# Four unit-matrix products into an unread bank behind each step of the last three half chunks

## The chip, the cores and the metric

The kernel runs on one core of a Trainium2 chip, whose five engines work side by side: TensorE (PE in the profile, with its weight loads as PEld), VectorE (DVE), ScalarE (ACT), GpSimd (POOL) and SyncE (SP), which only issues DMAs here. Each engine takes its instructions strictly in the order in which they are written, and starts one when the semaphores that it waits for have come. TensorE writes its results into eight banks of PSUM memory, from which VectorE and ScalarE read them.

The metric is the device time of one execution in microseconds. The profile also gives, for each stretch of time, the clock that TensorE was granted, as a share of its full speed; that share is called the clock here.

## The reference

A recurrence over 768 time steps for 4 x 8 heads of dimension 40, and behind it a gated MLP on its output:

```python
for t in range(S):
    y[:, :, t] = np.einsum('bhd,bhde->bhe', rt, state)
    Sa = np.einsum('bhde,bhe->bhd', state, at)
    state_decay = state * wt[:, :, None, :] - np.einsum('bhd,bhe->bhde', Sa, bt)
    state = state_decay + np.einsum('bhd,bhe->bhde', vt, kt)
...
h = x @ w_in
h = 0.5 * h * (1.0 + np.tanh(c * (h + 0.044715 * h ** 3)))
u, v = (h[..., :d_ff // 2], h[..., d_ff // 2:])
v_n = (v - mu) / np.sqrt(var + 1e-06) * g_ln
v_s = np.einsum('ts,bsd->btd', w_sg, v_n) + b_sg[None, :, None]
return (x + (u * v_s) @ w_out).astype(np.float32)
```

`x` is the recurrence's output, 4 x 768 x 320; `w_in` is 320 x 1024, `w_sg` 768 x 768, `w_out` 512 x 320.

## The kernel before

**Chunks.** The recurrence is worked in 12 chunks of 64 time steps (`NCH`, `C`). Within a chunk it becomes products of small matrices for each of the 4 batches, with a triangular inverse ahead of them. The state that goes from chunk to chunk lies in `sc`.

**Half chunks.** The function `half(c, hf, side)` writes one half of a chunk: two batches' steps of chunk `c`, and the output steps of two batches whose state steps came half a chunk earlier. Half number 2c + hf counts them; 22 and 23 are the halves of the last chunk (c = 11), and 24 holds only the last two batches' output steps. The steps are:

- `chain1`: TensorE makes `ru` from `at` and `vs`; ScalarE copies it to `rhsb`.
- `chain_t`: TensorE transposes the state into `tp`; ScalarE copies it to `s2`.
- `chain2`: TensorE multiplies `xt`, the inverse, by `rhsb` into the second part of the same `ru`; ScalarE writes the negative to `vu`.
- `chain3`: the new state (`sp`, left out in the last chunk), and `vu` transposed into `ut`; ScalarE copies it to `vut`.
- `chain4`: TensorE makes `pq` from `vut` and `rt`; VectorE masks it into `pqs`.
- `chain5`: TensorE makes `yp` from `pqs`, `kbt`, `s2` and `rt`; VectorE scales it into `yt`, and SyncE stores it.

Each step has a place, a number in `CH`; the steps and the list `side` are sorted by place and written in that order, and this is the order in which every engine works. `side` brings what lies between: the inverse (`gp`, `xp`, `xt`), the decoding of the MLP's weights from 64-bit floats into two 32-bit parts (`stg`, `sc`, `lt`, `wih`, `wil`, `woh`, `wol`: loads on SyncE, then ScalarE, five VectorE steps each, GpSimd), and in half 24 the first three products of the MLP (`hv`). In half 24 the steps on `w_out` fill VectorE's queue.

**Behind the halves** comes the MLP: `hv` and `hu` (the two sides of `h`), then `sg` (the product with `w_sg`), then `op` (the product with `w_out`), in an order given by `SEQ`.

**Banks.** `ps(name)` gives the next PSUM tile. From the second half of chunk 9 on all eight banks are in use (six in one pool, two in another). A step that takes a bank waits until the bank's last reader is done.

**Precision.** The recurrence's products are 32-bit floats; the profile shows two rows for each such product, and the built order one.

Of the kernel before, what the change touches and what calls it, by code (L numbers as in the profile page):

```python
# [69 lines left out]
REST = 8  # L70
SGS = (5, 3, 5, 6, 7, 8, 8, 11, 10, 11, 12, 11)
PO = 313.2
DECO = (332.0, 334.0, 336.0, 338.5, 340.5, 342.5, 344.5, 347.0)
DSTEPO = (-4.0, -1.0, 0.0, 0.7, 1.4, 2.4)
SGE = "GVGVGVGVVVGG"
# [44 lines left out]
def engines(tc):  # L120
    nc = tc.nc
    return tuple(InOrder(tc, e) for e in (nc.vector, nc.scalar, nc.gpsimd, nc.tensor, nc.sync))
# [6 lines left out]
def attention(tc, a, xd, flag, keep, ps, mlp=None):  # L129
# [3 lines left out]
    V, A, G, T, Q = engines(tc)  # L133
    with ExitStack() as ctx:

        def pool(nm, side):

            c = ctx.enter_context(ExitStack())
            return c.enter_context(tc.tile_pool(name=nm, bufs=1, side=side)), c.close

        st, _ = pool("at_static", "left")
        ring_b, _ = pool("at_ring_b", "left")
# [19 lines left out]
        ident = st.tile([128, 128], F32, name="ident")  # L162
        mask = st.tile([128, C], F32, name="mask")
        n = NP * (C + 1)
# [72 lines left out]
        def ent(c, b):  # L237
            return (4 * c + b) % RING
# [154 lines left out]
        def load_vb(c, f):  # L393
            if c < NCH:
                Q.dma_start(out=vss[f][0:64], in_=a["vb"][c, f])

        def load_vu(c, f):
            if c < NCH:
                Q.dma_start(out=vus[f][0:64], in_=a["vs"][c, f])

        def load_rv(c, f):
            if c < NCH:
                for h in range(2):
                    r = slice(D * h, D * h + D)
                    Q.dma_start(out=rts[f][r, :, h], in_=a["rt"][c, f, r])
                Q.dma_start(out=vuts[f][0:2 * D, :, :, 0], in_=a["vt"][c, f])

        def chain1(c, b):
            at, vs, rb = ats[ent(c, b)], vss[b // 2][:, b % 2], rhsb[b]
            ru = rus[b] = ps("ru")  # L410
            k = 128 if c else 64
            for p in range(NP):
                for h in range(2):
                    T.matmul(ru[64 * h:64 * h + 64, D * p:D * p + D], lhsT=at[0:k, p, h],
                             rhs=vs[0:k, p, h], start=True, stop=True, skip_group_check=True)
            A.copy(out=rb, in_=ru[:, 0:NP * D].rearrange("p (q x) -> p q x", x=D))

        def chain_t(c, b):
            if c:
                tp = ps("tp")  # L420
                for g in range(2):
                    T.transpose(out=tp[0:80, 128 * g:128 * g + 128], in_=scs[b][:, 2 * g:2 * g + 2], identity=ident)
                st2[b] = st.tile([128, 4, D], F32, name="s2", bufs=4)
                A.copy(out=st2[b][0:80], in_=tp[0:80, 0:256].rearrange("p (g x) -> p g x", x=C)[:, :, 0:D])

        def chain2(c, b):
            xt, ru, rb, vu = xts[c % 2], rus[b], rhsb[b], vus[b // 2][:, b % 2]
            for p in range(NP):
                for h in range(2):
                    r = slice(64 * h, 64 * h + 64)  # L430
                    T.matmul(ru[r, 160 + D * p:160 + D * p + D], lhsT=xt[r, 4 * b + p], rhs=rb[r, p],
                             start=True, stop=True, tile_position=(64 * h, 64 * h), skip_group_check=True)
            uv = ru[:, 160:320].rearrange("p (i g x) -> p i g x", i=2, g=2)
            for h in range(2):
                A.mul(out=vu[64:128, :, h], in_=uv[64 * h:64 * h + 64], mul=-1.0)

        def chain3(c, b):
            kbt, vu, vs, sc = kbts[ent(c, b)], vus[b // 2][:, b % 2], vss[b // 2][:, b % 2], scs[b]
            if c < NCH - 1:
                sp = ps("sp")  # L440
                for p in range(NP):
                    for h in range(2):
                        l0 = 2 * D * p + D * h
                        T.matmul(sp[64 * h:64 * h + 64, D * p:D * p + D], lhsT=kbt[:, l0:l0 + 64],
                                 rhs=vu[:, p // 2, h, p % 2], start=True, stop=True)
                cn = exs[ent(c, b)][:, :, C:C + 1]
                e = 64 + D
                ts = sp[0:e, 0:NP * D].rearrange("p (q x) -> p q x", x=D)
                V.tensor_tensor(out=ts, in0=ts, in1=sc[0:e], op=ALU.add)
                V.tensor_tensor(out=sc[0:e], in0=ts, in1=bc(cn[0:e], [e, NP, D]), op=ALU.mult)  # L450
                for h in range(2):
                    r = slice(64 * h, 64 * h + 64)
                    A.copy(out=vs[64:128, :, h], in_=sc[r])
            ut = ps("ut")
            for g in range(4):
                T.transpose(out=ut[0:80, C * g:C * g + C], in_=vu[64:128, g // 2, g % 2], identity=ident[64:128, 64:128])
            A.copy(out=vuts[b // 2][0:80, b % 2, :, 1], in_=ut[0:80, 0:256].rearrange("p (q t) -> p q t", q=4))

        def chain4(c, b):
            rt, vut = rts[b // 2][:, b % 2], vuts[b // 2][:, b % 2]  # L460
            pq = ps("pq")
            for g in range(4):
                T.matmul(pq[:, 128 * g:128 * g + 128], lhsT=vut[:, g], rhs=rt[:, :, g], start=True, stop=True)
            pqs = pqt[b] = st.tile([128, 2 * NP, C], F32, name="pqs", bufs=2)
            V.tensor_tensor(out=pqs, in0=pq.rearrange("p (q t) -> p q t", t=C),
                            in1=mask.unsqueeze(1).broadcast_to([128, 2 * NP, C]), op=ALU.mult)

        def chain5(c, b):
            kbt, rt, pqs = kbts[ent(c, b)], rts[b // 2][:, b % 2], pqt[b]
            yp = ps("yp")  # L470
            for p in range(NP):
                o = slice(C * p, C * p + C)
                for h in range(2):
                    l0 = 2 * D * p + D * h
                    T.matmul(yp[64 * h:64 * h + 64, o], lhsT=kbt[:, l0:l0 + 64], rhs=pqs[:, 4 * (p // 2) + 2 * h + p % 2],
                             start=True, stop=True, skip_group_check=True)
                for h in range(2 if c else 0):
                    T.matmul(yp[64 * h:64 * h + D, o], lhsT=st2[b][0:80, 2 * (p // 2) + h],
                             rhs=rt[0:80, p % 2, 2 * (p // 2) + h],
                             start=False, stop=True, skip_group_check=True)  # L480
            yt = st.tile([128, NP, C], F32, name="yt", bufs=2)
            V.tensor_tensor(out=yt, in0=yp[:, 0:256].rearrange("p (q t) -> p q t", t=C),
                            in1=exs[ent(c, b)][:, :, 0:C], op=ALU.mult)
            xv = xd[b, :, C * c:C * (c + 1)].rearrange("(q h e) t -> h e q t", h=2, e=D)
            for h in range(2):
                Q.dma_start(out=xv[h], in_=yt[64 * h:64 * h + D])

        def half(c, hf, side):

            p, q = 2 * hf, 2 * hf + 1  # L490
            o, r = 2 - 2 * hf, 3 - 2 * hf
            oc = c - 1 if hf == 0 else c
            st = []
            z = CH[hf]
            if c < NCH:
                if (c, hf) != (0, 0):
                    st += [(z[0], lambda: chain1(c, p)), (z[1], lambda: chain1(c, q))]
                st += [(2, lambda: load_vb(c + 1, hf)),
                       (z[2], lambda: chain_t(c, p)), (z[3], lambda: chain2(c, p)), (z[4], lambda: chain_t(c, q)),
                       (z[5], lambda: chain2(c, q)), (z[6], lambda: chain3(c, p)),  # L500
                       (z[7], lambda: (chain3(c, q), load_vu(c + 1, hf)))]
            if oc >= 0:
                st += [(z[8], lambda: chain4(oc, o)), (z[9], lambda: chain4(oc, r)),
                       (z[10], lambda: chain5(oc, o)), (z[11], lambda: (chain5(oc, r), load_rv(oc + 1, 1 - hf)))]
            for _, f in sorted(st + side, key=lambda x: x[0]):
                f()

# [104 lines left out]
class Mlp:  # L612
# [273 lines left out]
    def side(self, c, hf):  # L886

        def at(p, f):
            plan.append((p, f))

        plan = []
        if self.plan is None:
# [9 lines left out]
            for k in range(12):  # L902
                for i, d in enumerate(DSTEP[DEC[k][1]]):
                    at(max(PIN + 0.1, DEC[k][0] + d), lambda k=k, i=i: step(k, i))
            at(PO, self.open_out)
            outs = {}
# [5 lines left out]

            for k, p in enumerate(DECO):
                for i, d in enumerate(DSTEPO):
# [171 lines left out]
```

## Time and profile before

| what | value |
| --- | --- |
| time, median of 3 runs | 664.4 us (663.64 to 666.62) |
| the profiled execution's own time | 665.51 us |
| its span, first to last instruction | 663.8 us |
| instructions | 22411 |
| TensorE busy | 580.4 us, 87% |
| VectorE busy | 510.4 us, 77% |
| ScalarE busy | 391.8 us, 59% |
| GpSimd busy | 385.9 us, 58% |
| mean clock over the span | 0.900 |

The span is split into 40 slices of 16.6 us on the page, and the clock of each is given as one digit, in tenths. A row of a timeline has the start, the length, the engine, the line, the operation, what is written and read, the shapes, the number of instructions merged into it, and in brackets the engine's idle time before and who ended it. All engine calls go through one helper, so all rows have its line, and the names tell them apart.

### The profile page before, as it was taken

Reading aid. Unit: us, or ns where it says so; the run is one execution under the profiler, and the core shown is the slowest. Engines: PE = TensorE matmul, PEld = TensorE weight load, DVE = VectorE, ACT = ScalarE, POOL = GpSimd, SP = SyncE. Lnnn points to the kernel's source line nnn. Section 1 sums busy time; section 2 is a strip of 40 time slices with the busy share of each in tenths; the row PEclk is TensorE's granted clock in tenths of the full one; section 3 lists DMA queues with packets and bytes.
Section 4 is the critical chain, followed back from the end, with each engine's and each line's share of the span. In section 5 each row is a group of like instructions: output and inputs, shape, how many; then the busy total and the mean of one; then the engine's idle time right before and its main releaser. Section 6 shows DMA issues by size and latency. Waiting matters only on the chain.

```text
span 663.8 us, 22411 instructions
## 1 busy us (share of the span) xinstructions
PE 580.4 (87%) x8950; PEld 525.7 (79%) x8950; DVE 510.4 (77%) x1097; ACT 391.8 (59%) x1106; POOL 385.9 (58%) x869
## 2 busy tenths in 40 slices
PE   6547998989999899998978692969999999999996
PEld 5436787878888778887967682859999999999995
DVE  7875778989889898898777569788679668667732
ACT  5555687978878788797763744654245335424410
POOL 6588886787877878778782455464332433333321
PEclk8555599999999999999978676789999999999999
DMA  6722233443443433433344332331002002100001
GB/s 223 235 78 78 81 95 104 114 118 102 115 109 107 121 106 108 108 93 101 81 113 119 90 88 73 93 110 47 31 13 91 12 19 68 35 31 1 31 24 41
DMA packets 57617, 56.54 MB, mean 85 GB/s; under 512 B 35936, under 2 KB 47456, under 8 KB 57504
## 3 DMA queue, kind: packets, MB, share of 16 engines
q1 hardware_dynamic: 57504, 55.02, 28.9%
q8 instruction: 72, 1.18, 0.7%
q14 instruction: 41, 0.34, 0.2%
HBM read 47.14 MB, written 7.86 MB: 83 GB/s over the span
## 4 chain that ended last, share of the span: by engine, by line
PE 50%; DVE 24%; ACT 14%; issue 7%; DMA 3%; POOL 1%; SPq 1%; DVEq 0%; POOLq 0%; ACTq 0%
PE sg L115 14%; PE op L115 7%; PE hu L115 5%; PE hv L115 5%; PE ab L115 4%; DVE at L115 3%; PE pq L115 3%; DVE fixed L115 3%; PE sp L115 2%; PE ru L115 2%; ACT nts L115 2%; DVE ex L115 2%; ACT xt L115 2%; PE yp L115 2%; DVE kb L115 2%
## 5 line engine op out<-in xcount | busy, mean ns | idle before, releaser
L115 POOL TENSOR_TENSOR tg<-x,n 128x126 f32<-128x126 f32 (+21 forms) x348 | 127.9, 368 | 45.6 <-DVE n L115 7.2
L115 POOL TENSOR_TENSOR x<-x,tg 128x126 f32<-128x126 f32 (+21 forms) x348 | 133.4, 383 | 27.3
L115 POOL TENSOR_TENSOR gx<-g,gy 128x384 fp32r<-128x384 f32 x32 | 33.4, 1046 | 84.6 <-ACT gy L115 83.5
L115 PE MATMUL ab<-at,kb 64*64 64x64 f32 x1536 | 44.5, 248 | 30.6 <-DVE kb L115 17.2
L115 PE MATMUL sg<-wsh,vh 128*128 128x384 f32 x192 | 65.4, 340 | 4.3 <-ACT vh L115 4.3
L115 ACT ACTIVATE nts<-ab 32x256 f32<-32x256 f32 x192 | 62.0, 323 | 10.4 <-DVE at L115 8.0
L115 PEld LDWEIGHTS ab<-at,kb 64*64 64x64 f32 x1536 | 35.9, 155 | 40.4 <-ACT junk L115 14.0
L115 PE MATMUL sg<-wsh,vl 128*128 128x384 f32 x192 | 65.5, 341 | 1.9 <-POOL vl L115 1.9
L115 PE MATMUL sg<-wsl,vh 128*128 128x384 f32 x192 | 65.1, 339 | 0.0
L115 PE MATMUL pq<-rt,vut 128*128 128x128 f32 x384 | 60.5, 306 | 3.8 <-ACT vut L115 3.0
L115 PE MATMUL yp<-pqs,kbt 128*64 128x64 f32 x768 | 50.2, 236 | 14.6 <-DVE pqs L115 13.1
L115 ACT CAST gy<-g 128x384 fp32r<-128x384 f32 x32 | 16.4, 514 | 74.5 <-DVE g L115 74.5
L115 PEld LDWEIGHTS pq<-rt,vut 128*128 128x128 f32 x384 | 52.3, 211 | 7.0 <-ACT vut L115 3.1
L115 PEld LDWEIGHTS yp<-pqs,kbt 128*64 128x64 f32 x768 | 40.7, 147 | 18.0 <-DVE pqs L115 13.7
L115 ACT COPY vs<-sc 64x160 f32<-64x160 f32 x88 | 28.3, 321 | 38.6 <-DVE sc L115 37.7
L115 ACT CAST vh<-v 128x512 fp32r<-128x512 f32 x24 | 14.9, 621 | 55.2 <-DVE v L115 55.2
L115 PE MATMUL yp<-rt,s 80*40 80x64 f32 x704 | 46.4, 232 | 0.0
L115 DVE SCALAR_TENSOR_TENSOR g<-sg,gl,bt 128x384 f32<-128x384 f32 x32 | 19.7, 616 | 32.2 <-PE sg L115 28.4
L115 POOL TENSOR_TENSOR vl<-v,vh 128x512 fp32r<-128x512 f32 x24 | 31.3, 1305 | 22.7 <-ACT vh L115 22.7
L115 DVE TENSOR_TENSOR at<-ab,mask 64x256 f32<-64x256 f32 x96 | 35.9, 409 | 7.6 <-PE ab L115 7.3
L115 PE MATMUL ru<-rhsb,xt 64*64 64x40 f32 x768 | 32.3, 242 | 9.9 <-ACT xt L115 9.9
L115 POOL TENSOR_TENSOR rs<-rs,mhalf 128x1 f32<-128x1 f32 x24 | 13.4, 560 | 46.8 <-DVE rs L115 41.8
(135 smaller groups left out, 1658.9 us busy)
## 6 DMA issues: line engine op xcount, KB each, us to landing
main<-main SPq DMA_DIRECT2D x88, 160.8 KB
vu<-vs SPq DMA_DIRECT2D x24, 160.0 KB
vs<-vb SPq DMA_DIRECT2D x24, 160.0 KB
rt<-rt SPq DMA_DIRECT2D x48, 80.0 KB
vut<-vt SPq DMA_DIRECT2D x24, 160.0 KB
xd<-yt SPq DMA_DIRECT2D x96, 40.0 KB
xt<-xd SPq DMA_DIRECT2D x16, 192.0 KB
out<-y SPq DMA_DIRECT2D x16, 192.0 KB
```

What stands on the lines that cost most here:

```text
L115: return self.tc.keep_in_program_order(f(*a, **k))
```

## The change

A new function takes a bank and multiplies the unit matrix by itself into it, `n` times. In the halves 22, 23 and 24 it is put behind every step of the half's own list, at the step's place plus 0.001; the list `side` stays without it. That list also holds the place of a load (`load_vb`), which in half 22 and 23 gets its fill as well: 13, 13 and 4 fills of four products. Nothing reads the banks that they write.

```diff
+FILLED = (22, 23, 24)
+FILL = 4
...
+        def fill(n):
+
+            wp = ps("wp")
+            for _ in range(n):
+                T.matmul(wp[:, 0:128], lhsT=ident, rhs=ident, start=True, stop=True, skip_group_check=True)
+
...
                        (z[10], lambda: chain5(oc, o)), (z[11], lambda: (chain5(oc, r), load_rv(oc + 1, 1 - hf)))]
+            if 2 * c + hf in FILLED:
+                st += [(x + 0.001, lambda: fill(FILL)) for x, _ in st]
             for _, f in sorted(st + side, key=lambda x: x[0]):
                 f()
```

Only TensorE's order changes; the other engines' instructions are the same in the same order. Three places are shown. In these rows a number behind a name tells tiles of one name apart, and a bracket names the semaphores (`Activation` is ScalarE's, `PE` TensorE's own, `DMAHW` a DMA queue's).

TensorE in half 22, from the first `pq` to `chain2` of the first batch. Before:

```order
L115 MATMUL pq_7528<-rt1_125,vut1_130 128x128 [waits DMAHW0_49,DMAHW6_49,DVE_49,DMAHW7_49,PE_49,Activation_49]
L115 MATMUL pq_7528<-rt1_125,vut1_130 128x128 x3
L115 MATMUL tp_7537<-ident_92,sc0_120 80x128 x2
L115 MATMUL xp_7542<-xt1_90,gs0_119 32x32 [waits Activation_49]
L115 MATMUL xp_7542<-xt1_90,gs0_119 32x32 x31
L115 MATMUL tp_7577<-ident_92,sc1_121 80x128 [waits DVE_49]
L115 MATMUL tp_7577<-ident_92,sc1_121 80x128
```

Now:

```order
L117 MATMUL pq_7543<-rt1_125,vut1_130 128x128 [waits DMAHW6_49,DMAHW0_49,DMAHW7_49,DVE_49,Activation_49]
L117 MATMUL pq_7543<-rt1_125,vut1_130 128x128 x3
L117 MATMUL wp_7550<-ident_92 128x128 [waits Activation_49]
L117 MATMUL wp_7550<-ident_92 128x128 x3
L117 MATMUL tp_7557<-ident_92,sc0_120 80x128 [waits PE_49]
L117 MATMUL tp_7557<-ident_92,sc0_120 80x128
L117 MATMUL wp_7562<-ident_92 128x128 x4
L117 MATMUL xp_7567<-xt1_90,gs0_119 32x32 x32
L117 MATMUL tp_7602<-ident_92,sc1_121 80x128 [waits DVE_49]
L117 MATMUL tp_7602<-ident_92,sc1_121 80x128
```

`wp_7550` takes the bank that the last `ut` of the half before held; what it waits for on ScalarE is the copy of that `ut` into `vut`. `tp` and `xp` stand behind it.

TensorE in half 23, from `chain4` of one batch to `chain4` of the other. Before:

```order
L115 MATMUL pq_7736<-rt0_124,vut0_129 128x128 x4
L115 MATMUL ru_7711<-rhsb2_117,xt1_90 64x40 x8
L115 MATMUL ru_7724<-rhsb3_118,xt1_90 64x40 x8
L115 MATMUL tp_7778<-ident_92,sc2_122 80x128 x2
L115 MATMUL pq_7783<-rt0_124,vut0_129 128x128 x4
```

Now:

```order
L117 MATMUL pq_7816<-rt0_124,vut0_129 128x128 x4
L117 MATMUL wp_7823<-ident_92 128x128 x4
L117 MATMUL ru_7776<-rhsb2_117,xt1_90 64x40 x8
L117 MATMUL wp_7846<-ident_92 128x128 x4
L117 MATMUL ru_7794<-rhsb3_118,xt1_90 64x40 x8
L117 MATMUL wp_7866<-ident_92 128x128 x4
L117 MATMUL tp_7873<-ident_92,sc2_122 80x128 x2
L117 MATMUL wp_7878<-ident_92 128x128 x4
L117 MATMUL pq_7883<-rt0_124,vut0_129 128x128 x4
```

Four fills now stand between the two `pq`, and four more between the second `pq` and the first `yp`.

TensorE at the end of half 24, where the last `yp` is followed by the MLP's first `hu`. Before:

```order
L115 MATMUL yp_8085<-pqs_8048,kbt15_112 64x64 x2
L115 MATMUL yp_8085<-rt1_125,s2_7797 40x64 x2
L115 MATMUL hu_8133<-xh_7267,wih_6815 128x384 x3
L115 MATMUL hu_8133<-xh_7267,wil_6816 128x384 x3
L115 MATMUL hu_8133<-xl_7268,wih_6815 128x384 x2
```

Now:

```order
L117 MATMUL yp_8230<-pqs_8183,kbt15_112 64x64 x2
L117 MATMUL yp_8230<-rt1_125,s2_7902 40x64 x2
L117 MATMUL wp_8251<-ident_92 128x128 x4
L117 MATMUL hu_8283<-xh_7267,wih_6815 128x384 x3
L117 MATMUL hu_8283<-xh_7267,wil_6816 128x384 x3
L117 MATMUL hu_8283<-xl_7268,wih_6815 128x384 x2
```

One fill stands between the two.

## The prediction, before the run

> **What bounds the kernel now.** I read the page's head and slices first, then the stretches of the last half chunks, then TensorE's timeline in them, and last what ScalarE (ACT) and VectorE (DVE) do there.
>
> ```profile
> span 663.8 us, 22411 instructions
> PEclk8555599999999999999978676789999999999999
> ```
>
> The clock row is what matters: from slice 24 on the granted clock sags, and stays low for six slices of 16.6 us. The halves that the change fills lie there. By the names in the timeline they run from 361.38 (first `ru` of chunk 11) to 381.95, to 393.31, and to 417.59 (the first `hu`); the next two rows are the gated MLP.
>
> ```profile
> 361.38:381.95 20.57, 12.85 (x227) 11.48 (x224) 10.48 (x29) 13.18 (x36) 6.68 (x9) 0.73 0.35 99
> 381.95:393.31 11.36, 11.36 (x161) 10.34 (x157) 6.17 (x19) 5.99 (x19) 5.39 (x8) 0.59 0.35 95
> 393.31:417.59 24.28, 11.43 (x108) 9.87 (x105) 22.45 (x53) 9.36 (x27) 15.48 (x26) 0.74 0.23 65
> 417.59:447.07 29.48, 23.35 (x108) 20.78 (x106) 23.48 (x50) 17.30 (x39) 15.03 (x18) 0.85 0.36 106
> 447.07:663.80 216.73, 210.28 (x1153) 201.89 (x1153) 145.43 (x283) 78.56 (x159) 68.86 (x70) 0.99 0.11 35
> ```
>
> The columns are length, then busy time of PE, its weight loads, DVE, ACT, POOL, then clock. Three limits follow each other: in half 22 PE has 7.7 us of pauses, in half 23 it has none (at 0.59), in half 24 DVE is busy 22.45 of 24.28 us and PE less than half. Behind 447 PE is busy to the end, so what is late there ends late.
>
> ```profile
> 362.40:365.40 3.00, 0.06 (x3) 0.00 (x0) 1.03 (x4) 1.44 (x4) 0.00 (x0) 1.00 0.23 74
> 369.50:370.50 1.00, 0.00 (x0) 0.00 (x0) 0.39 (x2) 0.72 (x4) 0.92 (x3) 1.00 0.53 119
> 370.50:371.50 1.00, 0.00 (x0) 0.00 (x0) 1.00 (x3) 0.10 (x1) 0.51 (x1) 0.63 0.34 97
> 373.47:389.98 16.51, 16.51 (x193) 15.45 (x194) 8.24 (x22) 8.90 (x27) 7.20 (x11) 0.50 0.28 80
> 415.68:421.00 5.32, 5.32 (x43) 5.16 (x44) 4.27 (x10) 2.19 (x8) 3.68 (x8) 0.50 0.17 37
> 421.00:423.00 2.00, 2.00 (x11) 2.00 (x10) 1.76 (x3) 0.63 (x2) 0.00 (x0) 0.76 0.70 210
> ```
>
> A 3.00 us pause left the clock at 1.00; the next one began at 368.29 and the clock fell in it at about 370.8. Then PE ran 16.51 us without a pause at 0.50. That is the cold stretch that the fills could remove.
>
> **The change, part by part.**
>
> *Price of a fill.* Thirty fills of four 128x128 products are added (13, 13 and 4). The same shape in this kernel is `pq`, four products, eight rows:
>
> ```profile
> 361.38 1.08 PE L115 MATMUL ru<-vs,at 128*64 128x40 f32 x32
> 365.43 1.16 PE L115 MATMUL pq<-rt,vut 128*128 128x128 f32 x8 [2.97 <-ACT vut L115]
> 366.42 0.38 PE L115 MATMUL tp<-ident,sc 128*80 128x128 f32 x2
> 366.74 1.20 PE L115 MATMUL xp<-xt,gs 64*32 64x32 f32 x64
> 367.87 0.42 PE L115 MATMUL tp<-ident,sc 128*80 128x128 f32 x2
> 372.87 0.43 PE L115 MATMUL ru<-rhsb,xt 64*64 64x40 f32 x2 [4.58 <-ACT xt L115]
> 373.47 1.93 PE L115 MATMUL ru<-rhsb,xt 64*64 64x40 f32 x30 [0.17 <-ACT xt L115]
> ```
>
> From start to next start (365.43 to 366.42) a group costs 0.99 us at full clock. At half clock:
>
> ```profile
> 375.90 2.07 PE L115 MATMUL pq<-rt,vut 128*128 128x128 f32 x8
> 377.90 0.65 PE L115 MATMUL ut<-ident,vu 64*80 64x64 f32 x4
> ```
>
> 2.00 us. I take 0.99 and 2.00. Bounds: from below the streaming alone, by the nearest row that is wide,
>
> ```profile
> 398.66 0.84 PE L115 MATMUL hv<-wil,xh 128*128 128x512 f32 x3
> 399.34 0.62 PE L115 MATMUL hv<-wih,xl 128*128 128x512 f32 x2
> ```
>
> where three rows of 512 columns take 0.68 us, so 128 columns 0.057 and eight rows 0.45 us; from above 1.16 us, `pq`'s whole row, if each fill drained before the next instruction. `pq` is the nearest by far: same shape, type and count.
>
> The Trainium skill ("TensorE: Matmul & The Clock Gate", section "Back-to-back issue gap") gives about 81 ns for each 128-column matmul in a stream of weight loads and matmuls; eight would be 0.65 us, an estimate from that page, against the 0.99 us that this trace shows. It is one of the rivals, below.
>
> *Up to 373.47: the fills hide, nearly.* Half 22 opens with two `ru` and three fills: 361.38 + 2 x 0.5 + 3 x 0.99 = 365.35, and `pq` could not start before 365.43 anyway. Its new bank also waits for the first of the two DVE steps on `yp`, and the fill behind it takes the bank that the last `ut` held and waits for ACT's copy out of it, the third of these rows:
>
> ```profile
> 365.01 0.37 ACT L115 COPY vut<-ut 80x256 f32<-80x256 f32 x1
> 365.74 0.75 DVE L115 TENSOR_TENSOR yt<-yp,ex 128x256 f32<-128x256 f32 x2
> 367.89 0.37 ACT L115 COPY vut<-ut 80x256 f32<-80x256 f32 x1
> ...
> 372.25 1.17 ACT L115 COPY xt<-xp 32x512 f32<-32x512 f32 x2
> ```
>
> So `pq` starts at about 366.1 (365.74 and half of 0.75) and is through at 367.1, and PE stands until 368.26, with two `tp`, `xp` and two more fills queued behind that one: 368.26 + 3 x 0.99 + 1.13 (`xp`) + 2 x 0.32 (`tp`) = 373.0. `xp` itself ends at about 371.6, before ACT comes to copy it (372.25, held by a decode step of DVE), so `ru` still starts on ACT's time. **Nothing gained, nothing lost**, but the pauses are now 0.7 and 1.2 us, and by the rows above the clock should not fall.
>
> *From 373.47 on PE is the limit, and pays.* Until the second `pq` of half 23 ends there were 16.51 us at 0.50: 8.26 at full clock, a gain of 8.25. In the same stretch the order puts 14 fills: 14 x 0.99 = 13.86. The end moves from 389.98 to 373.47 + 8.26 + 13.86 = 395.59, **5.6 us late**. DVE stood waiting for just that:
>
> ```profile
> 390.02 0.69 DVE L115 TENSOR_TENSOR pqs<-pq,mask 128x512 f32<-128x512 f32 x1 [2.06 <-PE pq L115]
> ...
> 394.89 0.41 DVE L115 TENSOR_TENSOR yt<-yp,ex 128x256 f32<-128x256 f32 x1
> ...
> 414.95 0.68 DVE L115 TENSOR_TENSOR pqs<-pq,mask 128x512 f32<-128x512 f32 x1
> ```
>
> From there DVE needs 4.87 us to `yt`, so it comes to it at 400.5. `yp` is behind four more fills: before, PE took 2.33 us from 389.98 to the first `yp`'s end (about 392.3, half of the two that fill the time to 393.31); at the clock of 0.81 it had there, that is 1.9. 395.59 + 4 x 0.99 + 1.9 = 401.45. So `yt` moves from 394.89 to 401.5: **6.6 us**. DVE works in order, and every later decode step and MLP step stands behind it.
>
> *Half 24 carries it.* PE enters it at 401.45 + 2 x 0.99 + 0.93 = 404.4, 11.1 late, but there DVE is the limit and PE has slack: the first `hv` ends at 406.3, ACT reads it at 401.33 + 6.6 = 407.9; the others have more. So the delay stays at 6.6, not 11.1, and the last `pqs`, at 414.95 before, starts at 421.5. The fills there cost nothing, except the last:
>
> ```profile
> 415.68 1.98 PE yp L115 x32
> 417.66 2.87 PE hu L115 x8
> ...
> 420.62 0.50 ACT p L115
> ...
> 421.21 0.55 DVE q L115
> ```
>
> This is the chain. PE still pauses some 6 us before the last `yp`, so it is cold again, and a fill now stands between `yp` and `hu`: 2.00 us. By the row of 421.00 to 423.00 (0.76) the clock rose at about 421.96, 6.28 us after PE restarted; if it does so again, `yp` 1.98, fill 2.00, then 2.3 us of `hu` cold and the other 0.57 at double speed: `hu` ends 6.6 us after the restart in place of 4.9: **1.6 us**.
>
> **Sum:** 0 + 6.6 + 0 + 1.6 = 8.2 us. The profiled execution took 665.51 us (span 663.8), so 673.7. It lies 1.1 over the median of 664.4; I put the forecast against the median: **672.6 us**.
>
> Other parts: the bank numbers shift by 30 allocations; PE's new waits for its own earlier fills were over long before, but for one fill directly behind another in the same bank, in front of a pause. ACT, DVE, POOL and SP keep their order. The three loads and stores that half chunks issue stay where they are.
>
> **Rivals.**
>
> *Fills are cheap, no change.* The point is where 373.47 + 8.26 + 14f = 389.98, f = 0.59 us. With 0.65 us: 390.83 at `pqs`, 0.85 late, `yp` in time; the cold fill 1.3. Together 2.15 us: 666.6. Against it stands the 0.99 row; for it, that the four fills share one matrix, which no group in the trace does.
>
> *Faster.* At f = 0.45 the cold stretch's gain wins: `pqs` ends PE's work at 388.03, 1.95 us early, DVE follows. If the fills also held the clock over half 24, `yp` and `hu` would take half of 4.85, less a fill of 0.45: another 1.95 early. 664.4 - 3.9 = 660.5. It needs the lower bound and a clock held through the 6 us pause; the trace lost it in pauses of 4.6.
>
> *The clock falls all the same.* If bank waits add pauses, fills run at 2.00 us: three of them ahead of `ru` make it 4 us late, then 16.51 + 14 x 2.00 up to `pqs`, 32 us late, near 700 with the rest. The Trainium skill speaks for it (same page, "A second HAM failure mode: psum-queue depth-cycling"): cycling through banks lets the PE idle briefly, so that the clock oscillates. Here the pauses before 373 are shorter than the 3.00 us that kept it.
>
> *Half 24 follows PE, not DVE.* Then 11.1 + 1.6: 677.1; with f = 1.16, 14.5 + 1.9: 680.8.
>
> *It does nothing.* Were the unread products not issued, 664.4; the built order shows all 30 groups.
>
> **How the numbers follow.** Forecast with its own bounds, half 24 following PE among them (668 to 681): 0.77. Cheap fills 0.11, nothing issued 0.01, faster 0.06, cold fills 0.05. 0.5% (3.3 us) is about what a measurement of this kernel can tell from no change. Slower 0.82, same 0.12, faster 0.06. The range runs from the cheap fills to most of the PE-bound half: 666.0 to 679.5.
>
> **What would show it.** `wp<-ident` rows with some 0.99 us a group at full clock; a clock of 1.00 through half 22 and 23; half 23 longer than 11.36 us though warm; `pqs` waiting for PE near 395.6; half 24 still with DVE over 90% busy and shorter PE pauses; a cold fill before `hu`. It is wrong if a group costs under 0.6 us, if the clock still falls near 371, or if the MLP's start moves by much other than 8 us.

## The result and the profile after

| | before | changed |
| --- | --- | --- |
| time, median of 4 runs each on the same chip | 664.14 us (663.64 to 666.62) | 675.71 us (673.18 to 676.99) |
| the profiled execution's own time | 665.51 us | 676.76 us |
| mean clock over the span | 0.900 | 0.92 |

The changed kernel is slower: ratio 1.0146, with a 95% interval of 1.0106 to 1.0186, which is 7 to 12 us. A second measurement on another chip ("changed again", below) gave 1.0162 (1.0137 to 1.0187). Forecast were 672.6 us and a range of 666.0 to 679.5.

The page of the changed kernel, in the same rows as before, and with its chain of work:

```profile
span 675.0 us, 22891 instructions
PEclk9555599999999999999959999788999999999999
PE 60%; DVE 16%; ACT 15%; issue 6%; DMA 2%; POOL 1%; DVEq 0%; SPq 0%; POOLq 0%; ACTq 0%
PE sg L117 14%; PE hu L117 7%; PE op L117 6%; PE hv L117 6%; PE ab L117 6%; PE wp L117 4%; PE sp L117 4%; ACT nts L117 3%; PE ru L117 3%; PE pq L117 3%; DVE at L117 2%; ACT xt L117 2%; PE yp L117 2%; PE gp L117 2%; DVE fixed L117 2%
```

The clock row has lost most of its sag: slices 20 to 28, 978676789 before, now read 959999788. The fall in slice 21 (337 to 354 us) lies ahead of the first fill; then comes full clock, and the 788 is the end of half 24 and the start of the MLP. And yet the span is 11.2 us longer. The last row says why: `wp`, the product that nobody reads, stands on the chain that ended last with 4% of the span. An instruction without a reader is on that chain only because TensorE does its queue in order and was the bound.

The five stretches, cut nearly as before: first `ru` of chunk 11, last `yp` of half 22 done, first `hv`, first `hu`, and the gated MLP. Two cuts lie a little beside the earlier ones: the last fill of half 22 (1.09 us from 385.30) is counted with half 23, and the event that was at 447.07 is at 457.40 here, 0.6 us ahead of the last cut.

```profile
362.21:385.30 23.09, 21.79 (x322) 19.60 (x318) 10.19 (x28) 13.81 (x37) 7.79 (x11) 1.00 0.32 89
385.30:406.80 21.50, 21.50 (x272) 20.01 (x269) 10.07 (x26) 7.60 (x23) 7.91 (x12) 1.00 0.26 67
406.80:427.94 21.14, 15.13 (x140) 13.59 (x138) 18.97 (x47) 8.87 (x27) 12.94 (x25) 0.82 0.20 56
427.94:458.00 30.06, 23.62 (x109) 20.87 (x109) 22.39 (x46) 16.26 (x36) 13.58 (x14) 0.84 0.37 106
458.00:675.00 217.00, 210.56 (x1153) 202.17 (x1151) 144.15 (x281) 78.05 (x157) 68.85 (x70) 0.99 0.11 34
```

Halves 22 and 23 have a clock of 1.00 (0.73 and 0.59 before), as the change is built to give. Half 23 is nevertheless 21.50 us long in place of 11.36 (20.4 without that fill), and PE is busy for all of it: at 1.00 in place of 0.59 it has much more to do. Half 24 is still DVE's: 18.97 of 21.14 us, 90%.

TensorE's timeline of the changed kernel, at two places (start, length, then the row):

```profile
372.47 1.06 PE L117 MATMUL wp<-ident 128*128 128x128 f32 x8
373.46 0.30 PE L117 MATMUL ru<-rhsb,xt 64*64 64x40 f32 x2
374.06 0.66 PE L117 MATMUL ru<-rhsb,xt 64*64 64x40 f32 x14 [0.30 <-ACT xt L117]
374.65 1.16 PE L117 MATMUL wp<-ident 128*128 128x128 f32 x8
375.74 0.66 PE L117 MATMUL ru<-rhsb,xt 64*64 64x40 f32 x16
376.33 1.16 PE L117 MATMUL wp<-ident 128*128 128x128 f32 x8
...
424.30 0.48 PE L117 MATMUL yp<-pqs,kbt 128*64 128x64 f32 x4 [6.01 <-DVE pqs L117]
426.21 2.08 PE L117 MATMUL wp<-ident 128*128 128x128 f32 x8
...
430.64 0.73 PE L117 MATMUL hu<-xh,wih 128*128 128x384 f32 x3
```

From start to next start a fill takes 1.09 us with small products on both sides (374.65 to 375.74) and 0.99 us with one on one side only (372.47 to 373.46); the last, cold one is shown with 2.08 us. PE's pauses in the first group are gone, but for 0.30 us. VectorE's timeline of the changed kernel gives the milestones to compare:

```profile
366.32 0.75 DVE L117 TENSOR_TENSOR yt<-yp,ex 128x256 f32<-128x256 f32 x2
391.65 0.69 DVE L117 TENSOR_TENSOR pqs<-pq,mask 128x512 f32<-128x512 f32 x1 [5.81 <-PE pq L117]
397.91 0.69 DVE L117 TENSOR_TENSOR pqs<-pq,mask 128x512 f32<-128x512 f32 x1 [4.17 <-PE pq L117]
403.87 0.43 DVE L117 TENSOR_TENSOR yt<-yp,ex 128x256 f32<-128x256 f32 x1 [1.03 <-PE yp L117]
423.57 0.68 DVE L117 TENSOR_TENSOR pqs<-pq,mask 128x512 f32<-128x512 f32 x1
```

DVE waits for `pq` 5.81 and 4.17 us here, where it waited 2.92 and 2.06 us before (at 385.87 and 390.02). One more row of the kernel before is needed as the partner of the last TensorE row above, the second group of `hu`:

```profile
420.32 1.16 PE L115 MATMUL hu<-xh,wih 128*128 128x384 f32 x3
```

### The profile page after: what moved, and what is told of

It reads as the page before. It is cut to its first block, busy times and chain, and to the rows that moved or that the text cites. A ratio compares the mean times of both kernels' runs of the same rounds, so it can differ in the third digit from the quotient of the medians.

```text
span 675.0 us, 22891 instructions
## 1 busy us (share of the span) xinstructions
PE 603.4 (89%) x9190; PEld 547.1 (81%) x9190; DVE 509.2 (75%) x1097; ACT 392.0 (58%) x1106; POOL 385.5 (57%) x869
## 4 chain that ended last, share of the span: by engine, by line
PE 60%; DVE 16%; ACT 15%; issue 6%; DMA 2%; POOL 1%; DVEq 0%; SPq 0%; POOLq 0%; ACTq 0%
PE sg L117 14%; PE hu L117 7%; PE op L117 6%; PE hv L117 6%; PE ab L117 6%; PE wp L117 4%; PE sp L117 4%; ACT nts L117 3%; PE ru L117 3%; PE pq L117 3%; DVE at L117 2%; ACT xt L117 2%; PE yp L117 2%; PE gp L117 2%; DVE fixed L117 2%
## 5 line engine op out<-in xcount | busy, mean ns | idle before, releaser
L117 PE MATMUL ab<-at,kb 64*64 64x64 f32 x1536 | 43.8, 245 | 31.7 <-DVE kb L117 17.8
L117 ACT ACTIVATE nts<-ab 32x256 f32<-32x256 f32 x192 | 62.0, 323 | 10.3 <-DVE at L117 7.8
L117 PE MATMUL pq<-rt,vut 128*128 128x128 f32 x384 | 57.8, 297 | 1.0 <-DVE yt L117 0.9
L117 PE MATMUL yp<-pqs,kbt 128*64 128x64 f32 x768 | 48.2, 230 | 7.5 <-DVE pqs L117 6.0
L117 PEld LDWEIGHTS pq<-rt,vut 128*128 128x128 f32 x384 | 49.9, 202 | 4.0 <-DVE yt L117 1.4
L117 PE MATMUL yp<-rt,s 80*40 80x64 f32 x704 | 44.4, 226 | 0.0
L117 DVE TENSOR_TENSOR pqs<-pq,mask 128x512 f32<-128x512 f32 x48 | 32.7, 681 | 15.0 <-PE pq L117 15.0
L117 PEld LDWEIGHTS sg<-wsh,vh 128*128 128x128 f32 x192 | 36.9, 192 | 5.8 <-ACT vh L117 5.7
```

The source lines that it names most:

```text
L117: return self.tc.keep_in_program_order(f(*a, **k))
```

## The experiments

The theory: fills cost TensorE their full time on the stretch where it is the bound, and that is more than the held clock gives back. Rivals: the price is in waits for banks or in issuing, not in the products; the held clock alone would pay; the cold fill ahead of `hu` is the main loss. All kernels are variants of the changed one, and each is timed beside the kernel before, on the same chip. Since the executions of one program differ in when the clock rises, the traces are compared by VectorE's milestones, in microseconds behind the first `yt` of half 22 (start to start): the second `pqs` of half 23, the `yt` behind it, and the last `pqs`.

| run | time, median | ratio to before (95%) | second `pqs` | `yt` | last `pqs` |
| --- | --- | --- | --- | --- | --- |
| before | 664.14 | | 24.28 | 29.15 | 49.21 |
| before again | 666.41 (one) | | 20.56 | 27.39 | 48.10 |
| changed | 675.71 | 1.0146 (1.0106 to 1.0186) | 31.59 | 37.55 | 57.25 |
| changed again | 676.94 | 1.0162 (1.0137 to 1.0187) | 31.59 | 37.54 | 57.60 |
| six fills, pauses of half 22 | 666.11 | 1.0002 (0.9976 to 1.0029) | 21.26 | 29.72 | 49.85 |
| half 24 only | 666.69 | 0.9999 (0.9973 to 1.0026) | 24.28 | 29.17 | 50.06 |
| two products a fill | 670.28 | 1.0063 (1.0040 to 1.0086) | 27.05 | 31.91 | 52.96 |
| one thin product a fill | 670.02 | 1.0069 (1.0046 to 1.0091) | 27.28 | 32.14 | 52.71 |
| two fills in half 22 | 664.57 | 0.9978 (0.9959 to 0.9996) | 20.30 | 26.97 | 47.76 |
| 9 and 24 products in half 24 | 665.58 | 0.9992 (0.9973 to 1.0012) | 20.59 | 27.39 | 48.21 |
| 16 and 28 products in half 24 | 665.10 | 0.9980 (0.9954 to 1.0007) | 24.28 | 29.17 | 50.05 |
| eight products a fill | 698.18 (one) | | 49.55 | 59.08 | 79.67 |

In the three kernels whose fills lie in half 24 alone, the first two milestones are reached without any fill, so these executions stand beside "before" and "before again" as three more of the same program up to there. Of the five, three have the second `pqs` at 24.28 and two at 20.56 and 20.59: by this much one program's executions differ, and the comparisons below with "before" are with one of the first kind.

### Only the fills in the pauses of half 22

```diff
-FILLED = (22, 23, 24)
+FILLED = (22,)
...
-                st += [(x + 0.001, lambda: fill(FILL)) for x, _ in st]
+                st += [(x + 0.001, lambda: fill(FILL)) for x, _ in st if x < 5.2]
```

> Only the first six fills of half 22 stay, those that are written ahead of the 372.87 step; the other 24 are left out. Theory A (a fill costs PE about 1.0 us, and what the fills bring is a clock that does not fall at 371): the six hide in the pauses as they do in the changed kernel, the stretch of 16.5 us at half clock takes about 8.3, and VectorE, which has 8.2 us of work there, follows by 5 to 8 us: 656.5 to 659.5 us. Rival B (the small products of the recurrence cannot hold the clock, only fills among them do): the clock falls again inside half 22 or 23, 661 to 665 us. Rival C (the loss is in the new waits for banks in half 22, not in the products): slower than before, 667 us or more.

No change was measured: 666.11 against 666.26 us. The gain that the theory expected isn't there, though the clock did what it was to do, without any fill behind 375.3. The windows of this kernel's trace:

```profile
375.00:385.00 10.00, 8.58 (x188) 7.71 (x186) 7.56 (x18) 6.63 (x20) 3.97 (x5) 1.00 0.19 58
385.00:398.00 13.00, 11.40 (x120) 9.26 (x117) 9.71 (x21) 5.56 (x17) 7.80 (x11) 1.00 0.39 104
```

So the kernel's own products, most of them small, held the clock here once it was up. Where the gain went shows in the milestones: the second `pqs` is 3.0 us earlier than before, the `yt` behind it 0.6 us later. TensorE's and then VectorE's timeline of this kernel:

```profile
365.48 0.61 PE L117 MATMUL ru<-vs,at 128*64 128x40 f32 x16
...
375.28 1.28 PE L117 MATMUL ru<-rhsb,xt 64*64 64x40 f32 x32
```

```profile
365.64 0.75 DVE L117 TENSOR_TENSOR yt<-yp,ex 128x256 f32<-128x256 f32 x2
...
386.90 0.68 DVE L117 TENSOR_TENSOR pqs<-pq,mask 128x512 f32<-128x512 f32 x1
388.89 0.95 DVE L117 TENSOR_SCALAR sc<-sc 128x256 f32<-128x256 f32 x2 [1.31 <-ACT sc L117]
392.44 0.62 DVE L117 TENSOR_SCALAR sc<-sc 128x256 f32<-128x256 f32 x2 [1.74 <-ACT sc L117]
395.36 0.41 DVE L117 TENSOR_TENSOR yt<-yp,ex 128x256 f32<-128x256 f32 x1
```

Two things ate it. PE came into half 22 at 365.48 here (at 361.38 in the trace of before), so six fills no longer fitted ahead of `chain2`, which starts 9.64 us behind the first `yt` (375.28 - 365.64) in place of 7.13. And DVE, having its `pqs`, stands 1.31 and 1.74 us for a decode step of ACT. This kernel's chain of work says for what the second of these steps waits (start, length, piece):

```profile
387.13 0.72 POOL lt L117
...
388.93 2.97 DMA stg<-w_out
391.98 0.44 ACT sc L117
```

GpSimd frees a staging buffer, SyncE's load into it takes 2.97 us, and only then do ACT and DVE go on. TensorE has no part in these pieces.

### Only the fills of half 24

```diff
-FILLED = (22, 23, 24)
+FILLED = (24,)
```

> Only the four fills of half 24 stay. Theory A: three of them hide in PE's pauses there, the last one stands between the last yp and the first hu at half clock and costs 1.5 to 2 us: 665.5 to 666.2 us, and the first hu group ends 6.5 us after the last yp begins (4.9 before). Rival (this fill warms the clock early enough to pay for itself): within 0.5 us of before, hu ends under 5.5 us after yp begins.

The time can't tell 1.5 us from nothing here; the trace can. TensorE's rows of this kernel at the end of half 24:

```profile
416.22 0.48 PE L117 MATMUL yp<-pqs,kbt 128*64 128x64 f32 x4 [7.03 <-DVE pqs L117]
418.13 2.08 PE L117 MATMUL wp<-ident 128*128 128x128 f32 x8
...
422.12 0.70 PE L117 MATMUL hu<-xh,wih 128*128 128x384 f32 x3
```

From the last `yp` to the second group of `hu` it is 422.12 - 416.22 = 5.90 us, against 420.32 - 415.68 = 4.64 before and 430.64 - 424.30 = 6.34 in the changed kernel. In the second execution of the changed kernel ("changed again") it is 431.50 - 426.07 = 5.43. The cold fill thus costs 0.8 to 1.7 us, by when the clock rises. It is a loss, but the small one.

### Two products a fill, and eight

```diff
-FILL = 4
+FILL = 2
```

> All 30 fills, but two products each in place of four, so about 0.52 us each at full clock; same banks, same waits. Theory A: at 0.59 us a fill the gain of the clock and the products' price cancel at the second mask of half 23, so this one is about 1 us early there, and about 0.8 us late by the cold fill before hu: 662.5 to 665.5 us. Rival C (the waits for banks are what costs): as slow as the changed kernel, 672 to 677 us. Rival D (the clock brings nothing on the path, the products cost half): 668 to 671 us.

It was slower by 4 us, where the time of before or a little less was expected: half the products don't turn the loss into a gain. The time lies in the range of the rival by which the clock brings nothing on the path (668 to 671), but the trace speaks against that rival. Of the 2.8 us by which the second `pqs` is later, 1.7 are there when `chain2` starts (374.59, 8.85 us behind the first `yt`), and only 1.1 come between, where 14 fills of 0.45 us for the products alone (below) would have added 6.3 had the clock brought nothing. TensorE's first fill inside `chain2`, and VectorE's second `pqs`, of this kernel:

```profile
375.78 0.71 PE L117 MATMUL wp<-ident 128*128 128x128 f32 x4
392.79 0.69 DVE L117 TENSOR_TENSOR pqs<-pq,mask 128x512 f32<-128x512 f32 x1 [2.39 <-PE pq L117]
```

With eight products:

```diff
-FILL = 4
+FILL = 8
```

> The changed kernel with eight products in each fill in place of four. If the price of the products on TensorE is all, at 1.03 us for four (measured in the changed kernel), the 14 fills between chain2 and the second pqs of half 23 add another 14.4 us, and six fills in half 22 no longer fit in the pauses and add 4 to 6: second pqs 50 to 52 us after the first yt of half 22 (31.6 in the changed kernel, 24.3 in the profile of before), the fall of the clock not before half 24, 697 to 704 us in all. If VectorE or a wait took a share of the 11 us, the addition is clearly smaller.

The time came out inside the expected range, the second `pqs` 0.5 us below its own (49.55 against 50 to 52). TensorE's rows of this kernel, where one fill now takes 1.98 us (379.24 to 381.22), and VectorE's second `pqs`:

```profile
379.24 2.05 PE L117 MATMUL wp<-ident 128*128 128x128 f32 x16
381.22 0.66 PE L117 MATMUL ru<-rhsb,xt 64*64 64x40 f32 x16
...
415.01 0.69 DVE L117 TENSOR_TENSOR pqs<-pq,mask 128x512 f32<-128x512 f32 x1 [7.75 <-PE pq L117]
```

These two and the changed kernel make a line. From the start of the first fill inside `chain2` to the start of the second `pqs`, with 14 fills between and the clock at full speed, it took 17.01 us with two products (375.78 to 392.79), 23.26 with four (374.65 to 397.91) and 35.77 with eight (379.24 to 415.01). Two more products in each of the 14 fills cost 6.25 us, four more 12.51: **0.223 us a product both times**. The waits and the count of fills are the same in all three, so the products are what is paid for. Drawn on to no product, the line gives 23.26 - 14 x 0.894 = 10.7 us, in which the turns between products and fills are still contained. The kernel before took 15.6 us for this (390.02 minus 374.40, which is 373.47 plus half of `ru`'s 1.86). The held clock is thus worth 4.9 us to PE in this stretch beside the turns, and the products of a fill may cost 4.9 / 14 = 0.35 us before it loses. Two products cost 0.45 us, four 0.89. This is counted from the first trace of before. In the second one, where the clock rose earlier, the same stretch took 11.9 us (387.52 minus 375.64, found in the same way): against that execution the held clock is worth 1.2 us, and the products of a fill may cost no more than 0.09 us.

### One thin product a fill

One product of 32 x 4 in each fill: the same places, the same banks, next to no work.

```diff
-FILL = 4
+FILL = 1
...
-                T.matmul(wp[:, 0:128], lhsT=ident, rhs=ident, start=True, stop=True, skip_group_check=True)
+                T.matmul(wp[0:32, 0:4], lhsT=ident[:, 0:32], rhs=ident[:, 0:4], start=True, stop=True, skip_group_check=True)
```

> All 30 fills take their banks and wait as in the changed kernel, but each is one product of 32 columns of the unit matrix with 4 columns, under 0.1 us. Theory A: neither price nor warmth, the clock falls near 371 as before, 663 to 666 us. Rival C (bank waits): 667 us or more. Rival E (any activity in the pauses keeps the clock): under 661 us with the clock at 1.00 through half 22.

It was slower by about 4 us, over what the theory expected and inside the range of the rival of the bank waits (667 or more). The clock fell all the same, some 4 us later than before, and TensorE's rows of this kernel show what each fill cost at half clock, 375.66 - 375.46 = 0.20 us, where under 0.1 was expected:

```profile
375.46 0.27 PE L117 MATMUL wp<-ident 128*32 128x4 f32 x2
375.66 0.65 PE L117 MATMUL ut<-ident,vu 64*80 64x64 f32 x4
```

14 of them make 2.8 us; the second `pqs` came 3.0 us later than before (27.28 against 24.28). No row behind one of these fills shows a wait for a bank, but a wait inside the 0.20 us can't be told from the issue of the two rows, so that rival is open for these 0.2 us a fill. It does not touch the price of the products above, where the number of fills is the same.

### Two fills, and fills in the pauses of half 24

Two fills behind the two `chain_t` of half 22, and nothing else:

```diff
-FILLED = (22, 23, 24)
+FILLED = (22,)
...
-                st += [(x + 0.001, lambda: fill(FILL)) for x, _ in st]
+                st += [(x + 0.001, lambda: fill(FILL)) for x, _ in st if 3.9 < x < 5.2]
```

> Only two fills stay, behind the two transposes of half 22, in the pause before the inverse comes; they should be through before 372.5. The earlier run with six of them held the clock to 398 but began chain2 2.4 us later than before, and gained nothing at yt. Theory F (the clock is worth little on the path, because the decoding of the MLP's weights, load to buffer to ScalarE, VectorE, GpSimd and the buffer's release, takes the limit as soon as PE is faster): second pqs of half 23 up to 6 us earlier, but yt at 394.9 at most 2 us earlier: 662.5 to 666 us beside a before of 664 to 666, ratio 0.996 to 1.000. Rival G (the six fills' 2.4 us hid a gain that is worth the whole of PE's time): yt 5 us earlier, ratio under 0.993.

This is the fastest kernel of the study beside its own before: 0.9978, with an interval that ends at 0.9996. But its trace doesn't show it to be the fills. TensorE's rows of this kernel:

```profile
370.84 0.31 PE L117 MATMUL ru<-rhsb,xt 64*64 64x40 f32 x2 [1.47 <-ACT xt L117]
...
373.09 2.08 PE L117 MATMUL pq<-rt,vut 128*128 128x128 f32 x8
```

Some 2 us behind a pause of 1.47 us the clock fell all the same, as the 2.08 us of `pq` show; it rose again near 380. The milestones are within 0.5 us of those of the next kernel, which has no fill before half 24:

```diff
-FILLED = (22, 23, 24)
+FILLED = (24,)
+FILLS = {10.76: 9, 13.17: 24}
...
-                st += [(x + 0.001, lambda: fill(FILL)) for x, _ in st]
+                st += [(x + 0.001, lambda x=x: fill(FILLS[x])) for x, _ in st if x in FILLS]
```

> No fills in halves 22 and 23. In half 24 nine products behind the second pq (2.3 us in a pause of 4.6) and 24 behind the first yp (6.2 us in a pause of 8.3), none between the last yp and hu. Theory: the clock is held until the last yp, which takes 1.0 in place of 2.0 us, and the first hu 1.5 in place of 2.9: the MLP starts 2.4 us earlier, ratio 0.996 to 0.997. Rival (the clock falls in the 3 us that remain, or the 24 run at half clock and end late): between 1.000 and 1.005.

> As the run with 9 and 24 products in the pauses of half 24, with 16 and 28. There the nine ended 4.2 us ahead of the first yp, the clock fell and the 24 began at 0.5; 1.9 us of pause were left before the last yp, which ran at 1.00, but hu behind it was cold again. With 16 the pause before the first yp is some 2.2 us: if the clock holds there, the 28 take 7.2 us and leave 2 us; from the last yp to the second hu group some 3.0 to 3.8 us in place of 4.6: ratio 0.996 to 0.999. Rival (28 products begin cold and end after the mask): the last yp late by up to 1 us, ratio 1.000 to 1.003.

The second of these has 16 and 28 products in the same two places. Neither changed the time beyond its interval, where 0.996 to 0.997 was expected of the first. TensorE's rows of the one with 9 and 24:

```profile
401.55 0.48 PE L118 MATMUL yp<-pqs,kbt 128*64 128x64 f32 x4 [4.18 <-DVE pqs L118]
...
403.46 7.24 PE L118 MATMUL wp<-ident 128*128 128x128 f32 x48
412.58 0.34 PE L118 MATMUL yp<-pqs,kbt 128*64 128x64 f32 x4 [1.88 <-DVE pqs L118]
...
413.65 1.31 PE L118 MATMUL hu<-xh,wih 128*128 128x384 f32 x3
...
416.36 1.04 PE L118 MATMUL hu<-xh,wih 128*128 128x384 f32 x3
```

The last `yp` is warm and last `yp` to second `hu` takes 3.78 us in place of 4.64. But the clock fell again inside the first `hu`, some 1 us behind a pause of only 1.88 us, as this window of its trace shows (0.50):

```profile
414.00:417.00 3.00, 3.00 (x11) 3.00 (x10) 2.94 (x9) 1.98 (x6) 2.27 (x7) 0.50 0.17 37
```

With 28 products the pause was 3.44 us, `yp` was cold again and the same distance 4.63 us, where 3.0 to 3.8 were expected; its ratio still fell inside the expected 0.996 to 0.999, but not by that step. Pauses of 1.88 and 3.44 us ahead of the last `yp` were thus still too long in these two runs, and the warm `yp` brought 0.9 us.

### Both kernels again

> The changed kernel as it is, on this chip, for comparison with the runs of the same call: 1.012 to 1.019 times before. The second pqs of half 23 7 to 8 us later than before when both are counted from the first yt of half 22, and the first hu group 1.5 to 2 us longer after the last yp.

> The kernel before, for its trace on this chip: the same clock of 0.5 from 371 to 391 and from 405 to 421; the time at which the clock rises around 354 may differ by some us from execution to execution, and with it the start of half 22 on PE (361.4 in the profile of before, 364 to 367 in the four runs so far), with the first yt of half 22 at 365.3 to 366.4 all the same.

The changed kernel's milestones repeat to 0.35 us. Those of the kernel before don't, and that is a natural experiment. A clock of 0.5 until 391 was expected, as in the first trace; in this execution it had risen by 383, as a window of it shows (0.80), and VectorE's timeline follows:

```profile
382.00:384.00 2.00, 2.00 (x59) 1.98 (x56) 1.90 (x8) 1.06 (x3) 0.32 (x1) 0.80 0.52 126
```

```profile
387.52 0.69 DVE L115 TENSOR_TENSOR pqs<-pq,mask 128x512 f32<-128x512 f32 x1 [0.21 <-PE pq L115]
389.22 0.96 DVE L115 TENSOR_SCALAR sc<-sc 128x256 f32<-128x256 f32 x2 [1.01 <-ACT sc L115]
...
394.35 0.41 DVE L115 TENSOR_TENSOR yt<-yp,ex 128x256 f32<-128x256 f32 x1
```

With an earlier clock and no fill at all, the second `pqs` is 3.7 us earlier than in the first trace (20.56 against 24.28), `yt` 1.8 us, the last `pqs` 1.1 us. Of what PE gains, DVE gives a part back in waits for `sc` (1.01 us here and 0.38 further on), the decode loop shown above. The kernel with 9 and 24 products, without a fill up to there, repeats it (20.59, 27.39, 48.21). So a clock that rises 8 us earlier and costs nothing is worth one to two microseconds here.

## Why the prediction was right, point by point

Right were the sign, the place and the mechanism; the size was short. By the first profiled execution of each the delay built up as follows (changed minus before, at the same event):

| step | predicted | measured | from |
| --- | --- | --- | --- |
| up to `chain2`: the fills hide | 0 | 0.6 | `ru` 374.06 against 373.47 |
| to the second `pqs` | 5.6 | 7.3 | 397.91 against 390.02, less 0.6 |
| to `yt` | 1.0 | 1.1 | 403.87 against 394.89: 9.0 |
| half 24 carries it | 0 | -0.4 | 423.57 against 414.95: 8.6 |
| cold fill ahead of `hu` | 1.6 | 1.7 | 430.64 against 420.32: 10.3 |
| from there to the end | 0 | 0.9 | span 675.0 against 663.8: 11.2 |

The rows hang on which execution of before is taken: against the second one, by the milestones, the second `pqs` would be 11.0 us late (31.59 against 20.56) and the last `pqs` 9.2.

**"The fills hide, nearly."** Right for this trace: PE reached half 22 at 362.21 in place of 361.38, ahead of any fill, the first `yt` is 0.6 us later (366.32 against 365.74), and `chain2` follows it by the same time (373.46 - 366.32 = 7.14 us, 7.13 before). That it fitted so well was luck of the execution, though. In the second execution of the changed kernel PE came in 2.45 us ahead of the first `yt` (365.28), in place of 4.11, and `chain2` began 7.35 us behind it; in the run with six fills PE came in 0.16 us ahead, and the same fills cost 2.5 us.

**"From 373.47 on PE is the limit, and pays."** Right, and here lies the mis-sized term. The sum was 8.26 + 14 x 0.99. From 374.06 to the end of the second `pq` at 397.87 (its row in the chain of work has 0.89 us from 396.98) were 23.81 us, of which the 14 fills took 14.37: **1.03 us each, not 0.99**, since each turn between a fill and a small product costs 0.1 us: 0.90 us between wide products (395.92 to 396.82), 0.99 with one such turn, 1.09 with two. The rest took 9.44 us, **not 8.26**. The halving was wrong: `pq` halved (2.00 to 0.89 us), but 16 rows of `ru` took 0.59 us at full clock, where half of the cold 1.86 us for 30 rows would be 0.50 us for 16; `yp`, 64 rows from 378.48 to 381.95, went from 3.47 us to 2.14 (twice the 1.07 us between 382.08 and 383.15). With fills among them small products ran in about 60% of their cold time. Part of that is the turns: in the second trace of before, at full clock and without fills, 32 rows of `ru` took 1.06 us (385.12 to 386.18) against 1.87 cold in the first (385.76 to 387.63), 57%. The two errors, 1.2 and 0.5 us, make the 1.7 us.

**"`yt` moves by 6.6", "half 24 carries it".** The steps held: `yt` waited for `yp` (1.03 us), DVE was 90% busy in half 24, and PE's extra lateness vanished in its slack. The rival in which half 24 follows PE would have added some 4.5 us between `yt` and the last `pqs`; the distance shrank by 0.4 instead.

**The cold fill.** 1.7 us in this trace, 1.3 in the kernel with fills in half 24 alone and 0.8 in the second execution of the changed kernel, so that 1.6 was met so closely is luck too. The prediction's own terms come to 1.7 (1.98 + 2.00 + 2.3 + 0.29 = 6.57, less 4.85), not 1.6.

**The clock row.** The prediction lets the sag begin with slice 24. The row falls first in slice 21 (7, from 332 to 348 us), ahead of the filled halves; no term of the sum uses this.

**The end.** The last 0.9 us come from the clock's phase in the MLP. The windows of the first ten microseconds behind the same `sg`, of before and then of the changed kernel:

```profile
447.07:457.07 10.00, 10.00 (x52) 10.00 (x53) 9.28 (x17) 5.66 (x14) 3.44 (x3) 0.89 0.33 99
```

```profile
457.40:467.40 10.00, 10.00 (x47) 10.00 (x48) 9.27 (x17) 5.66 (x14) 3.43 (x3) 0.80 0.34 102
```

Five rows of `sg` fewer were done there, at 0.80 in place of 0.89. No fill is near. Whether the shift by 10 us set that phase, or chance, was not tried.

**The rivals.** "Cheap fills" needed 0.59 us and "faster" 0.45 us a fill; a fill cost 1.03 us, twice what the stretch could bear: (16.51 - 9.44) / 14 = 0.51 us, turns and all. What the Trainium skill's figure for 128-column matmuls ("TensorE: Matmul & The Clock Gate", section "Back-to-back issue gap") gives for eight rows, an estimate of 0.65 us, is not what these runs show: 0.89 us for eight rows even fill behind fill. "The clock falls all the same" didn't happen: 1.00 through both halves, with banks taken in turn by fills and steps; the section "A second HAM failure mode: psum-queue depth-cycling" of that page of the Trainium skill finds no support here. Two conditions of these rivals were wrong besides the price: the break-even of 0.59 us stood on the halving, and "faster" took PE's gain for DVE's, of which the decode loop leaves a third to a half (1.1 to 1.8 of 3.7 us).

**Still open.** Whether the 0.2 us of a thin fill are issue or a hidden wait for a bank; what makes the kernel with two fills 0.2% faster; and what sets the time at which a cold clock rises (below).

## What to carry to other kernels

Work that only keeps the clock up was paid for at its full price, 0.223 us a product, where that engine was the bound; it was free only in a pause, and a pause that is free in one execution may be gone in the next. Before buying a faster clock, ask what is late next: here the loop of load, ScalarE, VectorE and GpSimd took back half and more of what TensorE won. And halve for a doubled clock only products that are wide; small ones still took 57 to 62% of their time here. Trace the kernel before more than once, too: what a held clock is worth was 4.9 us against one execution of it and 1.2 against another.

## What was not expected of the hardware

- **How long PE's work takes to raise the clock differs from execution to execution.** In five executions of the same program up to there PE was shown busy without a pause from the second `ru` of `chain2` on, at 0.50. The clock rose 17.8 us behind it in the kernel before (373.47 to 391.2), and 17.8 and 17.9 us in the kernels with four fills and with 16 and 28 products in half 24; but 8.1 us in "before again" (374.71 to 382.8) and 8.2 us with 9 and 24 products. Behind the last `yp`, `hu` raised it within 6.3 us of PE's restart in the kernel before. Once up it stayed up among small products (1.00 from 375 to 398, by the windows of the run with six fills). What sets the time isn't shown.
- **No one length of pause loses the clock.** Behind the first `ru` of half 22 a pause of 2.97 us kept it in the kernel before, and one of 3.16 us at the same place lost it in "before again", where `pq` then took 2.08 us. The clock also fell 1 us behind a pause of 1.88 us with 9 and 24 products, and 2 us behind one of 1.47 us with two fills.
- **One program's executions differ in the clock by several microseconds of TensorE's work** (second `pqs` 24.28 and 20.56 us behind the same `yt`), while their own times are 665.51 and 666.41 us. DVE's loop hides part of it, 2.6 of the 3.7 us by the last `pqs`.
